# Chunked attention and a capacity-limited expert layer: wider rows for queries, keys and values, and zeros written beside the attention

## The chip, the cores and the metric

The kernel runs on one core of one Trainium2 chip. The metric is the device time of one execution in microseconds (us), here the median of three executions. Inside the core, TensorE (PE in the profile; its weight loads are PEld) multiplies and transposes, VectorE (DVE), ScalarE (ACT) and GpSimd (POOL) copy and compute elementwise, and SyncE (SP) issues nearly all transfers. The transfers run on 16 DMA engines.

## The reference

Two stages, in float32. The first is attention in chunks of 32 queries, each over 8 memory tokens and a window of up to 56 tokens; the second sends each token to its best expert, of 8, and keeps at most 80 tokens an expert.

```python
# q, k, v: (4, 8, 768, 64); mem_k, mem_v: (4, 8, 8, 64); per chunk c of 32 tokens:
k_full = concat(mem_k, k[max(0, 32c - 16) : min(768, 32c + 40)])      # v_full likewise
out[chunk c] = softmax(q_c @ k_full.T / 8) @ v_full
# x: (3072, 512), the heads of a token side by side
logits = x @ w_gate; e = argmax(logits); gw = softmax(logits)[e]
# of the tokens of expert e the 80 with the largest gw are kept
out[kept] = gw * (relu(x[kept] @ w1[e]) @ w2[e])                      # all other rows are zero
```

Since at most 640 of the 3,072 rows get a value, the kernel writes zeros to the whole output first and scatters the kept rows over them.

## The kernel before

**Tiling of the attention.** There are 16 pairs of heads, each with 768 tokens. A pair is done in two halves of 384 tokens, which makes 32 units (`units`, `NU`). A unit has four groups of 96 queries (`GQ`, `NG`), three chunks each, and a group sees 128 keys (`WK`): 8 of the memory and 120 tokens. So the values of a unit are, for each of two heads and four groups, 128 rows (8 of memory, 120 of tokens) of 64 numbers and a one; the one makes the sum of the weights come out of the same matmul.

**Loading.** `load_q` and `load_k` bring a pair's 768 tokens in as 96 partitions of eight tokens (`T0`), for two heads, so each partition gets two runs of 2,048 bytes. GpSimd copies that into the order in which TensorE can turn it (`kh`, L318; `qh`, L294), TensorE turns it (L330, L301), and VectorE or ScalarE moves the result from PSUM to `kT` and `qT` (L335, L304). Since the windows begin 16 tokens before a group and the memory takes eight, a key's first column lies two partitions over; one of four transposes uses a shifted identity (`shift`) for this. `load_v` brings in rows 8 to 127 of `vw` (L250), one transfer a head, in rows of 64 numbers or 256 bytes. Ahead of this GpSimd sets the ones (L242) and copies the memory's values into rows 0 to 7 (L243).

**Order.** The loop over `NU` units is written out. In step i TensorE makes the scores of unit i+1 (L765), turns a coming pair's keys or queries, turns the result of unit i-1 (L364), and multiplies unit i by its values (L346). Between these lie pieces of the ranking of tokens (`steps`), one a step. `in_order` fixes the order on every engine as it is written. SP's transfers are in that order too: in step i, the keys or queries two pairs on, the values of unit i+6, a finished block of `x` to DRAM (`xd`, L370), and, in three of four steps from i = 4 on, a piece of 512 KB of expert weights (L184, from the list `slow`, 20 pieces of five weights).

**After the attention** come the rest of the ranking, which fills `idx_g` and `idx_s`, then the eight experts. SP writes the zeros behind the last block of `x`: 12 pieces of 512 KB (`nothing`, L194), then the weights that are still missing, 44 pieces. Both go through `paced`, which keeps three pieces under way. The 16 expert weights have nine places (`WR`); the loads from w9 on wait for a matmul to leave their place. `run_experts` gathers an expert's rows of `xd` (L924), turns them (L936), multiplies by the first weight (L957) and the second (L971), and scatters the rows (L1019).

Of the kernel before, what the change touches and what calls it, by code (L numbers as in the profile page):

```python
# [12 lines left out]
F32 = mybir.dt.float32  # L13
# [5 lines left out]
PSUM = bass.MemoryType.PSUM  # L19

CHUNK = 32
LEFT = 16
RIGHT = 8
GQ = 96
NG = 4
HT = NG * GQ
T0 = 8
JG = GQ // T0
MS = 8
WK = 128  # L30
# [4 lines left out]
def _ap(ap, extra, dims):  # L35
    return bass.AP(tensor=ap.tensor, offset=ap.offset + extra, ap=dims)
# [26 lines left out]
def kernel(  # L63
# [13 lines left out]
    nc = tc.nc  # L77
    B, H, S, D = q.shape
# [13 lines left out]


    WR, WR0, WR2 = 9, 2, 2
    assert D == 64 and G == 2 * NG and NC == 96 and HT % 128 == 0 and mem_k.shape[2] == MS == T0
# [13 lines left out]
    xd = dram.tile([N, DM], F32, name="xd")  # L109

    ident = const.tile([128, 128], F32, name="ident")
    shift = const.tile([NC + 2, NC + 2], F32, name="shift")
# [88 lines left out]
    class Attention:  # L201


        def __init__(self, es, ps_t, ld):
            self.ld, self.nld = ld, 0
            self.ps_t = ps_t
            pool = es.enter_context(tc.tile_pool(name="at", bufs=1))
            self.io = es.enter_context(tc.tile_pool(name="io", bufs=2))
            self.mem = pool.tile([128, NP, T0], F32, name="mem")
            self.qs, self.ks, self.qT, self.kT, self.vw, self.mv = {}, {}, {}, {}, {}, {}  # L210
            self.kh = pool.tile([NC + 2, T0, 2, D], F32, name="kh")
            nc.gpsimd.memset(self.kh[NC : NC + 2], 0.0)

        def room(self):

            self.nld += 1
            return self.ld[:NC, self.nld % 4, :].rearrange("p (e x) -> p e x", e=2)

        def load_q(self, n):
            if n >= NP:  # L220
# [12 lines left out]
        def load_v(self, n, f):  # L233

            b, h = n // HP, 2 * (n % HP)
            vw = self.vw[n, f] = self.io.tile([128, 2, NG, D + 1], F32, name="vw", tag="vw", bufs=8)
            edge = f * (NG - 1) if (n, f) in ((0, 0), (NP - 1, 1)) else None
            if edge is not None:

                r = slice(96, 128) if f else slice(0, 32)  # L240
                nc.gpsimd.memset(vw[r, :, edge, :D], 0.0)
            nc.gpsimd.memset(vw[:, :, :, D], 1.0)  # L242
            nc.gpsimd.tensor_copy(  # L243
                vw[:MS, :, :, :D], self.mv[b][:, h : h + 2].unsqueeze(2).to_broadcast([MS, 2, NG, D])
            )
            t0 = HT * f - LEFT
            if edge is None:

                for e in range(2):
                    nc.sync.dma_start(  # L250
                        vw[MS:, e, :, :D], _ap(v[b, h + e], t0 * D, [[D, WK - MS], [GQ * D, NG], [1, D]])
                    )
                return
            g0 = int(edge == 0)
            for e in range(2):
                nc.sync.dma_start(
                    vw[MS:, e, g0 : g0 + NG - 1, :D],
                    _ap(v[b, h + e], (t0 + GQ * g0) * D, [[D, WK - MS], [GQ * D, NG - 1], [1, D]]),
                )
            t1 = t0 + GQ * edge  # L260
            lo, rows = MS + max(0, -t1), min(S, t1 + WK - MS) - max(0, t1)
            nc.sync.dma_start(
                vw[lo : lo + rows, :, edge, :D], _ap(v[b, h], max(0, t1) * D, [[D, rows], [SD, 2], [1, D]])
            )

        def load_mv(self, b):
# [1 line left out]
            nc.sync.dma_start(self.mv[b], _ap(mem_v[b, 0], 0, [[D, MS], [MS * D, H], [1, D]]))  # L268

        def load_mem(self, queue):  # L270
            mk = self.mk = self.io.tile([NP, T0, 2, D], F32, name="mk", tag="kT", bufs=5)
            for e in range(2):
                queue.dma_start(
                    mk[:, :, e, :], _ap(mem_k, e * MS * D, [[2 * MS * D, NP], [D, T0], [1, D]])
                )

        def turn_mem(self):

            pt = self.ps_t.tile([128, T0, NP], F32, name="pm", tag="t")
            for t in range(T0):  # L280
                nc.tensor.transpose(
                    pt[:, t, :], self.mk[:, t].rearrange("p e d -> p (e d)"), ident[:NP, :NP]
                )
            nc.vector.tensor_copy(self.mem, pt.rearrange("p t n -> p n t"))

        def turn_q(self, n, copies=(nc.gpsimd.tensor_copy,)):
            if n >= NP:
                return
            qT = self.qT[n] = self.io.tile([128, S], F32, name="qT", tag="qT", bufs=5)

            qh = self.io.tile([NC, T0, 2, D], F32, name="qh", tag="turn", bufs=1)
            for e, copy in enumerate(copies):
                c = slice(0, 2) if len(copies) == 1 else slice(e, e + 1)
                copy(  # L294
                    qh.rearrange("p t e d -> p e t d")[:, c],
                    self.qs[n].rearrange("p e (t d) -> p e t d", d=D)[:, c],
                )
            for t0 in range(0, T0, 4):
                pt = self.ps_t.tile([128, 4, NC], F32, name="pq", tag="t")
                for t in range(4):  # L300
                    nc.tensor.transpose(  # L301
                        pt[:, t, :], qh[:, t0 + t].rearrange("p e d -> p (e d)"), ident[:NC, :NC]
                    )
                nc.scalar.copy(  # L304
                    qT.rearrange("p (x t) -> p x t", t=T0)[:, :, t0 : t0 + 4], pt.rearrange("p t x -> p x t")
                )

        def put_mk(self, n):
# [4 lines left out]
        def turn_k(self, n, spread=nc.gpsimd.tensor_copy):  # L313
            if n >= NP:
                return
            kT = self.kT[n] = self.io.tile([128, G, WK], F32, name="kT", tag="kT", bufs=5)
            kh = self.kh
            spread(  # L318
                kh[:NC].rearrange("p t e d -> p e t d"), self.ks[n].rearrange("p e (t d) -> p e t d", d=D)
            )  # L320
            if n:
                self.put_mk(n)
            win = kT[:, :, MS:].rearrange("p g (j t) -> p g j t", t=T0)
            for t0 in range(0, T0, 4):


                pt = self.ps_t.tile([128, 512], F32, name="pk", tag="t")
                for t in range(4):
                    lo, rows = 2 * (t > 0), NC + (2, 0, 0, 1)[t]
                    nc.tensor.transpose(  # L330
                        pt[:, NC * t + lo : NC * t + lo + rows],
                        kh[:rows, t0 + t].rearrange("p e d -> p (e d)"),
                        (shift if t == 0 else ident)[:rows, :rows],
                    )
                nc.vector.tensor_copy(  # L335
                    win[:, :, :, t0 : t0 + 4],
                    _ap(pt, 0, [pt.ap[0], [JG, G], [1, (WK - MS) // T0], [NC, 4]]),
                )

        def values(self, n, f, P, out):  # L340
# [347 lines left out]
    W.given[WR0] = wpool.tile([128, 4, F], F32, name="ld", tag=f"w{WR0}", bufs=1)  # L688

    with ExitStack() as actx:  # L690
        ps_t = actx.enter_context(tc.tile_pool(name="ps_t", bufs=2, space=PSUM))
# [13 lines left out]
        at.load_mv(0)  # L705
        at.load_v(0, 0)
        make_identity(nc, ident)
        nc.gpsimd.tensor_copy(shift[:, 2:], ident[: NC + 2, :NC])
        nc.gpsimd.tensor_copy(shift[:, :2], ident[: NC + 2, NC : NC + 2])
# [116 lines left out]
        at.load_q(3)  # L826
        at.load_v(0, 1)
        at.load_v(1, 1)
        for i in range(NU):
            n, f = units[i]  # L830
            r = i // HP
# [20 lines left out]
            if later:  # L852
                later.popleft()()
            if i == NU - 2:
                lp = ps_t.tile([128, 512], F32, name="lp", tag="t")
# [199 lines left out]
    with tc.If(redo[1] > 0):  # L1055

        with ExitStack() as actx:
            wk = actx.enter_context(tc.tile_pool(name="wk2", bufs=2))
            gt = actx.enter_context(tc.tile_pool(name="gt2", bufs=1))
            ps_t = actx.enter_context(tc.tile_pool(name="ps_t2", bufs=2, space=PSUM))  # L1060
            ps_s = actx.enter_context(tc.tile_pool(name="ps_s2", bufs=2, space=PSUM))
# [8 lines left out]
            for i, (n, f) in enumerate((HP * b + c, f) for b in range(B) for f in range(2) for c in range(HP)):  # L1070
# [3 lines left out]
                if (c, f) == (0, 0):  # L1074
                    at.load_mv(n // HP)
                at.load_v(n, f)
                at.turn_k(n)
                if n == 0:
                    at.put_mk(n)
# [81 lines left out]
```

## Time and profile before

The time is 297.03 us (296.72 to 298.4 in three executions). The profiled execution spans 299.7 us.

| Engine | busy, us | share |
|---|---|---|
| PE | 249.9 | 83% |
| PEld | 217.6 | 73% |
| DVE | 107.6 | 36% |
| POOL | 88.9 | 30% |
| ACT | 81.7 | 27% |

An engine's share is an average over stages that differ, so it says little by itself. Three stages can be told apart by what the engines do: the attention to about 170 us, the end of the ranking to about 187 us, and the experts to the end. By transfer, the largest in the profile are 60 loads of weights of 512 KB, 60 loads of values of 120 KB, 16 of keys and 16 of queries of 384 KB, 12 pieces of zeros of 512 KB and 8 blocks of `xd` of 768 KB. The median time from issue to landing is 8.5 us for values and 6.6 us for keys.

### The profile page before, as it was taken

The page shows a single profiled execution, that of the slowest core. Times are in us where ns is not written, and L with a number is a line of the kernel's source. Part 1 is how long each engine was busy: PE and PEld are TensorE (multiplying, and loading weights), DVE is VectorE, ACT ScalarE, POOL GpSimd, SP SyncE. Part 2 cuts the span into 40 slices and gives each one's busy share as a digit, 9 for nine tenths or more (in the row PEclk, how much of TensorE's full clock was granted, in tenths as well). Part 3 has the DMA queues.
Part 4 walks back from the last instruction along what each step waited for, and adds up shares of the span by engine and source line. Part 5 has one row for each costly group of instructions (what it writes and reads, how often), then busy time and mean ns, then how long its engine had stood idle before and what let it go on. Part 6 is the DMA issues. An engine that isn't in the chain of part 4 may idle for free. (4 is left out here: it accounts for less than half of the span.)

```text
span 299.7 us, 11347 instructions
## 1 busy us (share of the span) xinstructions
PE 249.9 (83%) x5007; PEld 217.6 (73%) x5007; DVE 107.6 (36%) x282; ACT 81.7 (27%) x197; POOL 88.9 (30%) x209
## 2 busy tenths in 40 slices
PE   6799799777999796999799966999898939695980
PEld 6698688656887584887688844999897829695970
DVE  1232324745649443749365763010210101010030
ACT  2224145445455263365455410110010001010100
POOL 3566563614728125337011024110210200010121
PEclk9958879999799798799999965699999978997996
DMA  7999999999999999999937198998989989884001
GB/s 186 232 210 226 225 198 252 215 229 269 208 290 210 208 288 208 184 283 213 274 116 247 73 378 293 368 312 264 338 281 340 288 308 333 302 321 148 26 24 31
DMA packets 60454, 70.43 MB, mean 235 GB/s; under 512 B 34909, under 2 KB 34941, under 8 KB 60397
## 3 DMA queue, kind: packets, MB, share of 16 engines
q1 hardware_dynamic: 58381, 66.65, 85.5%
q0 software_dynamic: 1056, 2.62, 2.7%
q8 instruction: 41, 0.67, 1.0%
q10 hardware_dynamic: 960, 0.36, 0.6%
q14 instruction: 16, 0.13, 0.2%
HBM read 55.72 MB, written 13.89 MB: 232 GB/s over the span
## 5 line engine op out<-in xcount | busy, mean ns | idle before, releaser
L957 PE MATMUL hp<-xn,w 128*64 128x80 f32 x896 | 40.2, 255 | 12.1 <-DMA w<-in_moe_w_dram 9.9
L957 PEld LDWEIGHTS hp<-xn,w 128*64 128x64 f32 x896 | 37.8, 155 | 14.0 <-DMA w<-in_moe_w_dram 11.2
L765 PE MATMUL sp<-qT,kT 64*128 64x96 f32 x512 | 36.2, 282 | 5.5 <-issue 5.2
L773 ACT ACTIVATE P<-sp 128x384 f32<-128x384 f32 x64 | 28.0, 488 | 41.8 <-PE sp L765 41.8
L765 PEld LDWEIGHTS sp<-qT,kT 64*128 64x128 f32 x512 | 35.9, 202 | 3.8 <-issue 3.2
L346 PE MATMUL o<-vw,P 128*32 128x65 f32 x1536 | 32.5, 235 | 6.0 <-issue 4.1
L971 PE MATMUL yt<-hT,w 128*64 128x80 f32 x896 | 34.3, 234 | 1.9 <-issue 1.9
L346 PEld LDWEIGHTS o<-vw,P 128*32 128x32 f32 x1536 | 26.3, 118 | 12.7 <-issue 10.6
L971 PEld LDWEIGHTS yt<-hT,w 128*64 128x64 f32 x896 | 32.3, 137 | 4.0 <-issue 3.9
L961 ACT ACTIVATE hT<-hp 128x320 f32<-128x320 f32 x16 | 7.0, 438 | 98.7 <-PE hp L957 98.7
L1019 POOL DMA_INDIRECT out_dram<-y,idx_s x7 | 6.5, 934 | 81.9 <-DVE y L1018 66.5
L335 DVE COPY kT<-pk 128x480 f32<-128x480 f32 x32 | 19.8, 654 | 24.7 <-PE pk L330 24.6
L243 POOL COPY vw<-mv 8x512 f32<-8x512 f32 x32 | 20.6, 644 | 14.6 <-DMA mv<-in_mem_v_dram 14.6
L938 DVE COPY xn<-xp 128x320 f32<-128x320 f32 x8 | 3.9, 492 | 50.9 <-PE xp L936 50.9
L318 POOL COPY kh<-ld 96x1024 f32<-96x1024 f32 x15 | 15.5, 1035 | 18.3 <-PE more L534 6.6
L443 POOL TENSOR_TENSOR desc<-oh,masks 128x24 bf16<-128x24 bf16 x16 | 3.3, 228 | 58.9 <-DVE over_s L353 39.7
L516 DVE SCALAR_TENSOR_TENSOR less<-gbs,gw,behind 128x384 bf16<-128x384 f32 x21 | 19.2, 944 | 0.0
L301 PE MATMUL pq<-ident,qh 96*128 96x96 f32 x128 | 16.8, 283 | 2.4 <-POOL qh L294 2.1
L355 DVE TENSOR_TENSOR xr<-o,over_s 128x384 f32<-128x384 f32 x32 | 17.8, 558 | 1.1
L364 PE MATMUL xt<-ident,xr 128*128 128x128 f32 x96 | 17.9, 299 | 0.0
L294 POOL COPY qh<-ld 96x1024 f32<-96x1024 f32 (+1 forms) x16 | 16.4, 1028 | 4.1 <-DMA ld<-in_q_dram 4.1
L304 ACT COPY qT<-pq 128x384 f32<-128x384 f32 x32 | 14.4, 489 | 11.6 <-PE pq L301 11.4
(150 smaller groups left out, 330.7 us busy)
## 6 DMA issues: line engine op xcount, KB each, us to landing
w<-in_moe_w_dram SPq DMA_DIRECT2D x60, 512.0 KB, 5.8
vw<-in_v_dram SPq DMA_DIRECT2D x60, 120.0 KB, 8.5
ld<-in_k_dram SPq DMA_DIRECT2D x16, 384.0 KB, 6.6
ld<-in_q_dram SPq DMA_DIRECT2D x16, 384.0 KB, 6.7
xd<-xr SPq DMA_DIRECT2D x8, 768.0 KB, 7.3
out_dram<-zero SPq DMA_DIRECT2D x12, 512.0 KB, 5.1
ld<-in_moe_w_dram SPq DMA_DIRECT2D x4, 512.0 KB, 6.6
vw<-in_v_dram SPq DMA_DIRECT2D x4, 90.0 KB, 5.9
```

The source lines that it names most:

```text
L243: nc.gpsimd.tensor_copy(vw[:MS, :, :, :D], self.mv[b][:, h : h + 2].unsqueeze(2).to_broadcast([MS, 2, NG, D]))
L294: copy(qh.rearrange("p t e d -> p e t d")[:, c], self.qs[n].rearrange("p e (t d) -> p e t d", d=D)[:, c],)
L301: nc.tensor.transpose(pt[:, t, :], qh[:, t0 + t].rearrange("p e d -> p (e d)"), ident[:NC, :NC])
L335: nc.vector.tensor_copy(win[:, :, :, t0 : t0 + 4], _ap(pt, 0, [pt.ap[0], [JG, G], [1, (WK - MS) // T0], [NC, 4]]),)
L346: nc.tensor.matmul(out[32 * i : 32 * i + 32, e, t, :], lhsT=P[e][:, g, CHUNK * c : CHUNK * c + CHUNK], rhs=self.vw[n, f][:, e, g, :], star ...
L355: nc.vector.tensor_tensor(out=xr[:, :, 128 * c : 128 * c + 128].rearrange("p t (e d) -> p e t d", e=2), in0=o[:, :, :, :D], in1=over_s[:, ...
L364: nc.tensor.transpose(xt[:, 128 * t : 128 * t + 128], xr[:, t, 128 * c : 128 * c + 128], ident)
L516: nc.vector.scalar_tensor_tensor(out=self.less[:, i, :], in0=self.gb, scalar=self.gw[:, i : i + 1], in1=behind[:, 128 * (NT - 1 - i) : 128 ...
L765: nc.tensor.matmul(sp[e][:, g], lhsT=at.kT[n][r, NG * f + g, :], rhs=at.qT[n][r, HT * f + GQ * g : HT * f + GQ * g + GQ], start=False, sto ...
L773: nc.scalar.activation(P[i][e], sp[e], Act.Exp, scale=scale)
L957: nc.tensor.matmul(hp[j : j + 64, f, :], lhsT=w1[:, c, f1 : f1 + 64], rhs=xns[e][:, c, :], start=c == 0, stop=c == DK - 1,)
L971: nc.tensor.matmul(yt[j : j + 64, d, :], lhsT=w2[:, f, d * 128 + j : d * 128 + j + 64], rhs=hTs[e][:, f, :], start=f == 0, stop=f == FK - 1,)
```

## The change

There are four edits. Six tokens a partition (`T0 = 6`) make 128 partitions of keys and queries, with runs of 1,536 bytes, and three transposes a PSUM tile instead of four. The shift of the keys goes into the column at which a transpose writes, so `shift` is gone, and two fixed PSUM tiles `pt`, zeroed once, take the place of a rotating pair. The values come in as 128 rows, eight more than before, which lie under the memory's; the memory's values are copied over them afterwards, by `put_mv`, two steps ahead of use. The ones are written once, into eight fixed tiles (`rooms`). And in the steps from i = 4 on that issue no piece of weights, a piece of zeros is issued.

```diff
-T0 = 8
+T0 = 6
...
+            self.pt = [ps_t.tile([128, 512], F32, name=f"pt{i}", bufs=1) for i in range(2)]
+            for pt in self.pt:
+                nc.vector.memset(pt, 0.0)
...
-            self.kh = pool.tile([NC + 2, T0, 2, D], F32, name="kh")
-            nc.gpsimd.memset(self.kh[NC : NC + 2], 0.0)
+            self.kh = pool.tile([NC, T0, 2, D], F32, name="kh")
+            self.rooms = [pool.tile([128, 2, NG, D + 1], F32, name=f"vw{i}") for i in range(8)]
+            for vw in self.rooms:
+                nc.gpsimd.memset(vw[:, :, :, D], 1.0)
...
-            nc.gpsimd.memset(vw[:, :, :, D], 1.0)
-            nc.gpsimd.tensor_copy(
-                vw[:MS, :, :, :D], self.mv[b][:, h : h + 2].unsqueeze(2).to_broadcast([MS, 2, NG, D])
-            )
-            t0 = HT * f - LEFT
...
-                        vw[MS:, e, :, :D], _ap(v[b, h + e], t0 * D, [[D, WK - MS], [GQ * D, NG], [1, D]])
...
+            t0 = HT * f - LEFT - MS
...
+                    vw[:, e, g0:g1, :D],
+                    _ap(v[b, h + e], (t0 + GQ * g0) * D, [[D, WK], [GQ * D, g1 - g0], [1, D]]),
...
+        def put_mv(self, n, f):
+            b, h = n // HP, 2 * (n % HP)
+            nc.gpsimd.tensor_copy(
+                self.vw[n, f][:MS, :, :, :D],
+                self.mv[b][:, h : h + 2].unsqueeze(2).to_broadcast([MS, 2, NG, D]),
             )
...
-            for t0 in range(0, T0, 4):
-                pt = self.ps_t.tile([128, 4, NC], F32, name="pq", tag="t")
-                for t in range(4):
+            for t0 in range(0, T0, 3):
+                pt = self.pt[t0 // 3][:, 3 : 3 + 3 * NC].rearrange("p (t x) -> p t x", t=3)
+                for t in range(3):
...
-            for t0 in range(0, T0, 4):
...
-                pt = self.ps_t.tile([128, 512], F32, name="pk", tag="t")
-                for t in range(4):
-                    lo, rows = 2 * (t > 0), NC + (2, 0, 0, 1)[t]
+            for u0, step in ((0, NC), (3, NC + 1)):
...
+                pt = self.pt[u0 // 3]
+                for i in range(3):
+                    c = 3 + i * step - (u0 + i > 3)
                     nc.tensor.transpose(
-                        pt[:, NC * t + lo : NC * t + lo + rows],
-                        kh[:rows, t0 + t].rearrange("p e d -> p (e d)"),
-                        (shift if t == 0 else ident)[:rows, :rows],
+                        pt[:, c : c + NC], kh[:, (u0 + i + 2) % T0].rearrange("p e d -> p (e d)"), ident
                     )
...
         at.load_v(1, 1)
+        at.put_mv(*units[0])
+        at.put_mv(*units[1])
         for i in range(NU):
...
                 constants[i]()
+            if i + 2 < NU:
+                at.put_mv(*units[i + 2])
...
             if (i >= NU - 6 or i >= 4 and i % 4 < 3) and slow:
                 slow.popleft()()
+            elif i >= 4:
+                nothing.popleft()()
```

More of the change, by code (lines that the diff above doesn't have):

```diff
@@ L94 @@
     WR, WR0, WR2 = 9, 2, 2
-    assert D == 64 and G == 2 * NG and NC == 96 and HT % 128 == 0 and mem_k.shape[2] == MS == T0
+    assert D == 64 and G == 2 * NG and NC == 128 and HT % 128 == 0 and mem_k.shape[2] == MS
     assert N == B * S and DM == H * D and E == 8 and HP == DK == 4
@@ L111 @@
     ident = const.tile([128, 128], F32, name="ident")
-    shift = const.tile([NC + 2, NC + 2], F32, name="shift")
     masks = const.tile([128, mask_np.shape[1]], BF16, name="masks")
@@ L204, in __init__ @@
         def __init__(self, es, ps_t, ld):
-            self.ld, self.nld = ld, 0
-            self.ps_t = ps_t
+            self.ld, self.nld, self.nv = ld, 0, 0
+            self.pt = [ps_t.tile([128, 512], F32, name=f"pt{i}", bufs=1) for i in range(2)]
+            for pt in self.pt:
+                nc.vector.memset(pt, 0.0)
             pool = es.enter_context(tc.tile_pool(name="at", bufs=1))
             self.io = es.enter_context(tc.tile_pool(name="io", bufs=2))
-            self.mem = pool.tile([128, NP, T0], F32, name="mem")
+            self.mem = pool.tile([128, NP, MS], F32, name="mem")
             self.qs, self.ks, self.qT, self.kT, self.vw, self.mv = {}, {}, {}, {}, {}, {}
-            self.kh = pool.tile([NC + 2, T0, 2, D], F32, name="kh")
-            nc.gpsimd.memset(self.kh[NC : NC + 2], 0.0)
+            self.kh = pool.tile([NC, T0, 2, D], F32, name="kh")
+            self.rooms = [pool.tile([128, 2, NG, D + 1], F32, name=f"vw{i}") for i in range(8)]
+            for vw in self.rooms:
+                nc.gpsimd.memset(vw[:, :, :, D], 1.0)
         def room(self):
             self.nld += 1
-            return self.ld[:NC, self.nld % 4, :].rearrange("p (e x) -> p e x", e=2)
+            return self.ld[:NC, self.nld % 4, : 2 * T0 * D].rearrange("p (e x) -> p e x", e=2)
         def load_q(self, n):
@@ L235, in load_v @@
             b, h = n // HP, 2 * (n % HP)
-            vw = self.vw[n, f] = self.io.tile([128, 2, NG, D + 1], F32, name="vw", tag="vw", bufs=8)
+            vw = self.vw[n, f] = self.rooms[self.nv % 8]
+            self.nv += 1
             edge = f * (NG - 1) if (n, f) in ((0, 0), (NP - 1, 1)) else None
@@ L241, in load_v @@
                 nc.gpsimd.memset(vw[r, :, edge, :D], 0.0)
-            nc.gpsimd.memset(vw[:, :, :, D], 1.0)
-            nc.gpsimd.tensor_copy(
-                vw[:MS, :, :, :D], self.mv[b][:, h : h + 2].unsqueeze(2).to_broadcast([MS, 2, NG, D])
-            )
-            t0 = HT * f - LEFT
-            if edge is None:
-                for e in range(2):
-                    nc.sync.dma_start(
-                        vw[MS:, e, :, :D], _ap(v[b, h + e], t0 * D, [[D, WK - MS], [GQ * D, NG], [1, D]])
-                    )
-                return
+            t0 = HT * f - LEFT - MS
             g0 = int(edge == 0)
+            g1 = NG - int(edge == NG - 1)
             for e in range(2):
                 nc.sync.dma_start(
-                    vw[MS:, e, g0 : g0 + NG - 1, :D],
-                    _ap(v[b, h + e], (t0 + GQ * g0) * D, [[D, WK - MS], [GQ * D, NG - 1], [1, D]]),
-                )
[L260 to L263, printed above, removed]
+                    vw[:, e, g0:g1, :D],
+                    _ap(v[b, h + e], (t0 + GQ * g0) * D, [[D, WK], [GQ * D, g1 - g0], [1, D]]),
+                )
+            if edge is not None:
+                t1 = t0 + GQ * edge
+                lo, rows = max(0, -t1), min(S, t1 + WK) - max(0, t1)
+                nc.sync.dma_start(
+                    vw[lo : lo + rows, :, edge, :D], _ap(v[b, h], max(0, t1) * D, [[D, rows], [SD, 2], [1, D]])
+                )
+        def put_mv(self, n, f):
[3 more added lines that the diff above has]
+                self.mv[b][:, h : h + 2].unsqueeze(2).to_broadcast([MS, 2, NG, D]),
             )
@@ L270, in load_mem @@
         def load_mem(self, queue):
-            mk = self.mk = self.io.tile([NP, T0, 2, D], F32, name="mk", tag="kT", bufs=5)
+            mk = self.mk = self.io.tile([NP, MS, 2, D], F32, name="mk", tag="kT", bufs=5)
             for e in range(2):
                 queue.dma_start(
-                    mk[:, :, e, :], _ap(mem_k, e * MS * D, [[2 * MS * D, NP], [D, T0], [1, D]])
+                    mk[:, :, e, :], _ap(mem_k, e * MS * D, [[2 * MS * D, NP], [D, MS], [1, D]])
                 )
         def turn_mem(self):
-            pt = self.ps_t.tile([128, T0, NP], F32, name="pm", tag="t")
-            for t in range(T0):
+            pt = self.pt[1][:, : MS * NP].rearrange("p (t n) -> p t n", t=MS)
+            for t in range(MS):
                 nc.tensor.transpose(
@@ L297, in turn_q @@
                 )
-            for t0 in range(0, T0, 4):
-                pt = self.ps_t.tile([128, 4, NC], F32, name="pq", tag="t")
-                for t in range(4):
-                    nc.tensor.transpose(
-                        pt[:, t, :], qh[:, t0 + t].rearrange("p e d -> p (e d)"), ident[:NC, :NC]
-                    )
+            for t0 in range(0, T0, 3):
+                pt = self.pt[t0 // 3][:, 3 : 3 + 3 * NC].rearrange("p (t x) -> p t x", t=3)
+                for t in range(3):
+                    nc.tensor.transpose(pt[:, t, :], qh[:, t0 + t].rearrange("p e d -> p (e d)"), ident)
                 nc.scalar.copy(
-                    qT.rearrange("p (x t) -> p x t", t=T0)[:, :, t0 : t0 + 4], pt.rearrange("p t x -> p x t")
+                    qT.rearrange("p (x t) -> p x t", t=T0)[:, :, t0 : t0 + 3], pt.rearrange("p t x -> p x t")
                 )
@@ L318, in turn_k @@
             spread(
-                kh[:NC].rearrange("p t e d -> p e t d"), self.ks[n].rearrange("p e (t d) -> p e t d", d=D)
+                kh.rearrange("p t e d -> p e t d"), self.ks[n].rearrange("p e (t d) -> p e t d", d=D)
             )
@@ L323, in turn_k @@
             win = kT[:, :, MS:].rearrange("p g (j t) -> p g j t", t=T0)
-            for t0 in range(0, T0, 4):
-                pt = self.ps_t.tile([128, 512], F32, name="pk", tag="t")
-                for t in range(4):
-                    lo, rows = 2 * (t > 0), NC + (2, 0, 0, 1)[t]
+            for u0, step in ((0, NC), (3, NC + 1)):
+                pt = self.pt[u0 // 3]
+                for i in range(3):
+                    c = 3 + i * step - (u0 + i > 3)
                     nc.tensor.transpose(
-                        pt[:, NC * t + lo : NC * t + lo + rows],
-                        kh[:rows, t0 + t].rearrange("p e d -> p (e d)"),
-                        (shift if t == 0 else ident)[:rows, :rows],
+                        pt[:, c : c + NC], kh[:, (u0 + i + 2) % T0].rearrange("p e d -> p (e d)"), ident
                     )
                 nc.vector.tensor_copy(
-                    win[:, :, :, t0 : t0 + 4],
-                    _ap(pt, 0, [pt.ap[0], [JG, G], [1, (WK - MS) // T0], [NC, 4]]),
+                    win[:, :, :, u0 : u0 + 3],
+                    _ap(pt, 0, [pt.ap[0], [JG, G], [1, (WK - MS) // T0], [step, 3]]),
                 )
@@ L690 @@
     with ExitStack() as actx:
-        ps_t = actx.enter_context(tc.tile_pool(name="ps_t", bufs=2, space=PSUM))
+        ps_t = actx.enter_context(tc.tile_pool(name="ps_t", bufs=1, space=PSUM))
         ps_s = actx.enter_context(tc.tile_pool(name="ps_s", bufs=2, space=PSUM))
@@ L707 @@
         make_identity(nc, ident)
-        nc.gpsimd.tensor_copy(shift[:, 2:], ident[: NC + 2, :NC])
-        nc.gpsimd.tensor_copy(shift[:, :2], ident[: NC + 2, NC : NC + 2])
         nc.gpsimd.memset(wgc, 0.0)
@@ L854 @@
             if i == NU - 2:
-                lp = ps_t.tile([128, 512], F32, name="lp", tag="t")
+                lp = at.pt[0]
                 nc.tensor.matmul(lp[:, : NT * E], lhsT=zerob, rhs=zerob[:, : NT * E], start=True, stop=False)
@@ L1060 @@
             ps_t = actx.enter_context(tc.tile_pool(name="ps_t2", bufs=2, space=PSUM))
-            ps_s = actx.enter_context(tc.tile_pool(name="ps_s2", bufs=2, space=PSUM))
+            ps_s = actx.enter_context(tc.tile_pool(name="ps_s2", bufs=1, space=PSUM))
             ps_o = actx.enter_context(tc.tile_pool(name="ps_o2", bufs=1, space=PSUM))
@@ L1076 @@
                 at.load_v(n, f)
+                at.put_mv(n, f)
                 at.turn_k(n)
```

## The prediction

> **What bounds the kernel now.** I read the page's DMA rows first, then the busy time by stage, then the timelines of TensorE and SP in the stage where those disagree, then GpSimd's.
>
> ```profile
> PEclk9958879999799798799999965699999978997996
> DMA  7999999999999999999937198998989989884001
> GB/s 186 232 210 226 225 198 252 215 229 269 208 290 210 208 288 208 184 283 213 274 116 247 73 378 293 368 312 264 338 281 340 288 308 333 302 321 148 26 24 31
> DMA packets 60454, 70.43 MB, mean 235 GB/s; under 512 B 34909, under 2 KB 34941, under 8 KB 60397
> ```
>
> A digit is a slice of 7.5 us. The DMA engines are full in the attention (slices 2 to 20) at only 184 to 290 GB/s, nearly idle in slices 21 to 23, and full again at about 300 GB/s for the experts. So there is a hole of some 20 us in a resource that is short on both sides of it.
>
> ```profile
> core 0: us, PE busy (x) PEld busy (x) DVE busy (x) ACT busy (x) POOL busy (x), PEclk, DMA share, GB/s
> 28.00:157.00 129.00, 112.57 (x2300) 93.40 (x2300) 69.49 (x180) 59.27 (x145) 54.82 (x139) 0.92 1.06 228
> 190.00:280.00 90.00, 75.88 (x1810) 71.28 (x1807) 10.06 (x20) 6.57 (x15) 8.56 (x9) 0.93 0.86 288
> ```
>
> In the attention PE is busy 112.57 of 129 us and the DMA share is over 1[...]: two limits lie close together. In the experts PE is idle 14 us of 90, while all else but DMA rests. What ends that idle time is in PE's timeline (start, duration, what ran, and in brackets the idle time before it with its releaser):
>
> ```profile
> 244.07 0.53 PE L957 MATMUL hp<-xn,w 128*64 128x80 f32 x4 [3.14 <-DMA w<-in_moe_w_dram]
> 245.26 0.54 PE L957 MATMUL hp<-xn,w 128*64 128x80 f32 x4 [0.66 <-DMA w<-in_moe_w_dram]
> 246.53 5.92 PE L957 MATMUL hp<-xn,w 128*64 128x80 f32 x116 [0.73 <-DMA w<-in_moe_w_dram]
> 258.92 0.36 PE L957 MATMUL hp<-xn,w 128*64 128x80 f32 x4 [0.75 <-DMA w<-in_moe_w_dram]
> 260.81 4.23 PE L957 MATMUL hp<-xn,w 128*64 128x80 f32 x116 [1.53 <-DMA w<-in_moe_w_dram]
> 272.68 0.36 PE L957 MATMUL hp<-xn,w 128*64 128x80 f32 x4 [1.91 <-DMA w<-in_moe_w_dram]
> 274.21 5.74 PE L957 MATMUL hp<-xn,w 128*64 128x80 f32 x116 [1.17 <-DMA w<-in_moe_w_dram]
> ```
>
> The first weight matrices of the last three experts come late: the waits add to 9.89 us. After two of them the same 116 matmuls take 5.92 and 5.74 instead of 4.23 us, since the clock fell (6 in PEclk): 3.2 us more. So late weights cost **13.1 us**. Why they are late is in SP's timeline:
>
> ```profile
> 170.43 19.82 SPq L194 DMA_DIRECT2D out_dram<-zero  x12
> 191.05 78.15 SPq L184 DMA_DIRECT2D w<-in_moe_w_dram  x44
> ```
>
> The twelve pieces of zeros hold the queue for 19.82 us, 1.65 us each, ahead of every remaining weight; those then come at 78.15/44 = 1.78 us a piece. One stall in the attention concerns the change too:
>
> ```profile
> 73.18 0.73 POOL L243 COPY vw<-mv 8x512 f32<-8x512 f32 x1 [3.00 <-DMA mv<-in_mem_v_dram]
> 73.86 1.03 POOL L294 COPY qh<-ld 96x1024 f32<-96x1024 f32 x1
> 74.95 0.88 PE L301 MATMUL pq<-ident,qh 96*128 96x96 f32 x8 [2.13 <-POOL qh L294]
> ```
>
> GpSimd's copy of the memory's values waits for `mv`; the queries' copy queues behind it, and TensorE waits for that.
>
> [...]in its packet records the 2,048-byte packets take 127 ns on average in 28 to 150 us and 87 ns at 170 to 190, where zeros go out from 128 partitions. [...]in the attention PE stops six times for 0.4 to 3.0 us on "issue" in the middle of a group of matmuls[...].
>
> **The change part by part.** Where a sum has both ends, both go into the range.
>
> Zeros. From i = 4 on, the steps without a piece of weights are 7, 11, 15, 19, 23, 25 (the first 16 pieces are used up), 30 and 31: eight pieces move and four stay. The last three are issued after unit 31's values (145 us) and fall into the hole: free. At the end SP is done with zeros 8 x 1.65 = 13.2 us sooner, at 170.43 + 4 x 1.65 = 177 us. The next weights go into SBUF that the ranking's tiles may hold until about 182.4 us, when its last instruction ends on DVE. So the lead of the weights is between 191.05 - 182.4 = 8.7 and 13.2 us. The last late piece came at 274.2 us; without any stalls PE would want it at about 263 (274.2 less 9.89 of waits and 1.69 of slow matmuls). So about 11 us of lead removes everything, and 8.7 leaves some 2.5 us. Later weights wait for a place: w14 takes that of w5, free at 228 us, and I count it in at about 257 us, so the places don't bind. The gain is 9.5 to 13.1; I take **-12 us**.
>
> The five pieces within the attention add 5 x 256 packets of 2,048 bytes at 87 to 127 ns on 16 engines: 7.0 to 10.2 us of full DMA time.
>
> Queries and keys. A load is 256 packets of 1,536 instead of 192 of 2,048 bytes. On the line between 32 ns (256 bytes, same records) and 127 ns, 1,536 bytes take 100 ns: 32 loads go from 48.8 to 51.2 us, +2.4.[...] I take -5.
>
> Values. [...]averaged over 16 engines 6.7% more packets, at 32 ns some 61 us in all: 0 to +4. I take 0.
>
> So the attention's DMA demand grows by about 8.5 - 5 = 3.5 us, between -5 and +17. Does PE see it? Unit 14's values were issued by 62.6 us and landed 8.3 us later (median) at 70.9. GpSimd would come to `put_mv(14)`, behind `kT` in step 12, at about 82.5: 11.6 us of slack. Keys have more. So a small surplus is hidden[...]: **+1.5 us**.
>
> `put_mv`. A new wait: behind it on GpSimd is the next copy of keys or queries, and TensorE's transposes wait for those. With the slack above it costs nothing in the loop. It takes the place of the wait for `mv`: the stall of 2.13 us above goes, and the slower matmuls after it (xt 0.90 for 0.49, o 1.53 for 0.89 and those behind them, 1.5 us together). The two other waits for `mv` (3.3 and 4.85 us) lie beside "issue" stalls of PE that end as late: nothing. I take **-3 us**.
>
> Start. Four copies of memory values (0.60 us each) stand before the keys' copy at 13.49 us, for which PE idles 1.00 us and then runs at clock 0.73. They go behind it. But `put_mv(1)` then waits for values issued at 10.77 (landing about 19), and the next copy is needed for PE at 20.4. Two PSUM memsets come before the first matmuls, and the wait for `shift` goes. **-1.5 us** (0 to -2.5).
>
> Transposes. Queries: 8 x 83 to 6 x 110 ns by the spacing of matmul starts, nothing. Keys: 0.74 us for eight to six at 110 ns, 0.08 us, 16 times: **-1 us**. GpSimd's copies shrink with their elements (1.03 to about 0.78 us), and 32 memsets go: hidden, since GpSimd is idle 70%.
>
> Sum: -12 + 1.5 - 3 - 1.5 - 1 = -16; I round the small gains down to 15.5: 297.0 - 15.5 = **281.5 us**.
>
> **The rivals.** A: the attention becomes DMA-bound. For it: DMA never rests there. Against: 11 us of slack. With +8 instead of -4: 297 - 12 + 8 = 293. B: the weights' lead is lost, to SBUF that isn't free or to the nine places; then the experts give -6 and the attention -2: 289. C, slower: zeros at 127 ns[...], values at 6.7% more: +17 of DMA, all of it seen, since `put_mv` holds GpSimd[...]; the end gives only its lower bound of -9.5 and the small gains stay (-5.5): 297 + 17 - 9.5 - 5.5 = 299. D: [...]the attention, which loses its stalls: 275.
>
> **How the numbers follow.** 0.57 for the forecast (278 to 286), A 0.15, B 0.13, C 0.09, D 0.06. Reaching into A, B and D gives 275.5 to 293. Faster: the forecast, B, D and most of A, 0.87; within 0.5%: 0.04; slower: C, 0.09.
>
> **What would show it.** SP's zeros after 170 us are four, not twelve, and the weights follow by 182 us; L957's waits for weights fall from 9.9 us to under 2; POOL's waits for `mv` vanish and no longer ones for `vw` appear; the attention ends 2 to 6 us sooner. I am wrong if the experts still wait for weights, or if GpSimd waits over 5 us for values, or if PE's issue stalls grow.

## The result, and the profile after

The changed kernel takes **265.18 us** (261.76 to 265.68, four runs) against 297.71 us (296.72 to 302.32); the ratio is 0.8893, 95% interval 0.8794 to 0.8991. The forecast was 281.5 us, with 275.5 as the lower end: right in direction, but the gain is twice the 15.5 us that were forecast. Slower executions are left out of ratios and of the times in the table below, but the traces of the kernel before (301.62 us) and of e6 (278.19 us) are of such. The page of the profiled execution, of 263.6 us, in slices of 6.6 us:

```profile
PEclk9999999999999999999999557699999999999996
DMA  7999899999999999979192999979999998970110
GB/s 236 283 279 283 220 266 345 351 362 332 365 329 340 356 322 366 316 217 341 70 307 87 378 319 307 304 277 322 298 315 295 310 310 245 344 251 26 30 42 20
DMA packets 64598, 70.96 MB, mean 269 GB/s; under 512 B 37004, under 2 KB 45228, under 8 KB 64540
```

The DMA engines are as busy in the attention as before, but in slices 7 to 17 at 316 to 366 GB/s, where it was 184 to 290. PEclk stands at 9 through the attention, without the 7s and 8s of before. By stage (columns as before):

```profile
28.00:130.00 102.00, 97.84 (x2163) 81.54 (x2163) 64.28 (x176) 57.67 (x141) 46.98 (x108) 1.00 1.00 308
```

PE is busy 97.84 of 102 us, at full clock; it was 112.57 of 129 us at 0.92. SP's timeline, with the last store of `xd` before the change as the first line, and the group of the experts' first matmuls:

```profile
170.01 0.38 SPq L370 DMA_DIRECT2D xd<-xr  x1
```

```profile
144.15 0.38 SPq L370 DMA_DIRECT2D xd<-xr  x1
144.58 5.03 SPq L193 DMA_DIRECT2D out_dram<-zero  x4
150.46 82.21 SPq L183 DMA_DIRECT2D w<-in_moe_w_dram  x44
```

```profile
L961 PE MATMUL hp<-xn,w 128*64 128x80 f32 x896 | 35.0, 241 | 2.1 <-issue 1.5
```

Four pieces of zeros are left, the weights follow at once, and no wait for `w` remains (9.9 us before).

Two marks split the gain. From the first to the last unit's values (the first matmul of each, L346) it is 122.0 us instead of 144.1; the first comes at 20.4 instead of 24.1 us. From the last store of `xd` to the end it is 119.5 us instead of 129.7. So the attention, start included, gave some 26 us and the end 10.2. The two sum to 36 us, since the trace before is of a longer execution; the medians differ by 32.5. The forecast had 4 and 12. Hence the question of the experiments: what made the attention so much faster?

### The profile page after: what moved, and what is told of

Same layout as the page of the kernel before. It is cut to its first block, busy times and chain, and to the rows that moved or that the text cites. A ratio compares the mean times of both kernels' runs of the same rounds, so it can differ in the third digit from the quotient of the medians.

```text
span 263.6 us, 11283 instructions
## 1 busy us (share of the span) xinstructions
PE 232.0 (88%) x4943; PEld 202.7 (77%) x4943; DVE 104.4 (40%) x284; ACT 82.7 (31%) x197; POOL 80.3 (30%) x182
## 5 line engine op out<-in xcount | busy, mean ns | idle before, releaser
L771 ACT ACTIVATE P<-sp 128x384 f32<-128x384 f32 x64 | 27.9, 488 | 30.6 <-PE sp L763 30.6
L961 PE MATMUL hp<-xn,w 128*64 128x80 f32 x896 | 35.0, 241 | 2.1 <-issue 1.5
L961 PEld LDWEIGHTS hp<-xn,w 128*64 128x64 f32 x896 | 34.2, 144 | 2.5 <-issue 1.6
L346 PE MATMUL o<-vw,P 128*32 128x65 f32 x1536 | 28.7, 221 | 0.1
L346 PEld LDWEIGHTS o<-vw,P 128*32 128x32 f32 x1536 | 23.3, 109 | 5.6 <-issue 5.1
L335 DVE COPY kT<-pt 128x480 f32<-128x480 f32 x32 | 19.9, 668 | 18.0 <-PE pt L332 12.0
L305 ACT COPY qT<-pt 128x384 f32<-128x384 f32 x32 | 16.4, 580 | 8.4 <-PE pt L304 8.4
L355 DVE TENSOR_TENSOR xr<-o,over_s 128x384 f32<-128x384 f32 x32 | 17.8, 557 | 1.1
L366 ACT COPY xT<-xt 128x384 f32<-128x384 f32 x32 | 15.6, 489 | 4.3 <-PE xt L364 4.3
L981 DVE COPY ys<-yt 128x320 f32<-128x320 f32 x7 | 3.4, 492 | 32.4 <-PE yt L975 32.4
L319 POOL COPY kh<-ld 128x768 f32<-128x768 f32 x15 | 12.4, 825 | 12.0 <-issue 9.2
L304 PE MATMUL pt<-ident,qh 128*128 128x128 f32 x96 | 14.6, 283 | 1.1 <-DVE kT L335 1.1
```

What stands on the lines that cost most here:

```text
L304: nc.tensor.transpose(pt[:, t, :], qh[:, t0 + t].rearrange("p e d -> p (e d)"), ident)
L305: nc.scalar.copy(qT.rearrange("p (x t) -> p x t", t=T0)[:, :, t0 : t0 + 3], pt.rearrange("p t x -> p x t"))
L335: nc.vector.tensor_copy(win[:, :, :, u0 : u0 + 3], _ap(pt, 0, [pt.ap[0], [JG, G], [1, (WK - MS) // T0], [step, 3]]),)
L346: nc.tensor.matmul(out[32 * i : 32 * i + 32, e, t, :], lhsT=P[e][:, g, CHUNK * c : CHUNK * c + CHUNK], rhs=self.vw[n, f][:, e, g, :], star ...
L355: nc.vector.tensor_tensor(out=xr[:, :, 128 * c : 128 * c + 128].rearrange("p t (e d) -> p e t d", e=2), in0=o[:, :, :, :D], in1=over_s[:, ...
L366: nc.scalar.copy(xT, xt[:, :HT])
```

## The experiments

The theories: **rows** (96 rows of keys and 120 of values slow the DMA, 128 don't), with the rivals **computation** (fewer transposes, shorter copies, no wait for `mv`) and **packets** (the size of a packet counts). A load of keys or queries is said to have 96 or 128 rows by the partitions that it fills. "Values" below is the stretch from the first to the last unit's values, and "gaps" the sum of PE's pauses over 0.15 us in it. GB/s is the rate from 28 to 120 us. The 256-byte packet's mean time is from the trace's packet records, 28 to 150 us.

| kernel | time, us | values, us | gaps, us | GB/s | 256 B, ns |
|---|---|---|---|---|---|
| before | 297.03 | 144.1 | 16.6 | 233 | 32 |
| e1 zeros moved | 293.50 | 147.8 | 13.4 | 256 | 29 |
| e2 values in 128 rows | 292.14 | 136.1 | 11.4 | 253 | 28 |
| e3 keys and queries in 128 rows | 279.78 | 126.3 | 6.6 | 280 | 24 |
| e4 both, no zeros moved | 274.41 | 120.6 | 3.6 | 296 | 19 |
| after | 265.18 | 122.0 | 4.9 | 320 | 19 |
| e6 after, keys in 96 + 32 | 274.41 | 132.2 | 11.1 | 275 | 26 |
| e7 after, values in 120 + 8 | 273.90 | 126.4 | 9.1 | 280 | 22 |
| e8 before, `mv` early | 298.12 | 136.9 | 13.7 | 253 | 29 |
| e10 before, weights later (one execution) | 309.21 | 126.8 | 8.4 | 206 | 26 |
| e11 after, 11 MB more | 276.11 | 131.7 | 13.1 | 349 | 19 |
| e13 e3, keys in 96 + 32 | 293.93 | 140.6 | 16.1 | 247 | 29 |
| e14 after, longer copies | 265.57 | 123.1 | 4.4 | 314 | 19 |

Everything but the time is from one trace of each kernel. The kernel before was run again beside each group of experiments. Beside e1 to e4 one of its seven runs counts (292.5 us; all lie between 292.5 and 305.0), so these four are compared with each other and by their traces. Beside the others the runs that count took 297.5 to 302.5 us, so times of different groups compare only roughly.

**e1: the zeros alone.**

```diff
             if (i >= NU - 6 or i >= 4 and i % 4 < 3) and slow:
                 slow.popleft()()
+            elif i >= 4:
+                nothing.popleft()()
```

> The kernel before, with the eight pieces of zeros moved beside the attention and nothing else. Both theories agree on the end: the weights lead by some 13 us and the experts lose about 10 us. They also agree that the attention, whose DMA rate stays near 228 GB/s without wider rows, gets five pieces more (about 8 to 10 us of DMA time). If the DMA limits the attention, it gets 5 to 10 us longer and the total is 290 to 296 us; if its slack hides them, as I predicted, the total is about 286 us.

SP's timeline of e1:

```profile
171.29 0.38 SPq L370 DMA_DIRECT2D xd<-xr  x1
171.73 5.04 SPq L194 DMA_DIRECT2D out_dram<-zero  x4
177.61 2.44 SPq L184 DMA_DIRECT2D w<-in_moe_w_dram  x2
```

The weights start 6.3 instead of 21.0 us after the last store of `xd`, and the end from that store on takes 118.7 us instead of 129.7: -11.0. The values take 3.7 us more. So by the traces the move alone is worth some 7 us beside narrow rows; the times (293.50 us, against that one run of 292.5) don't resolve it.

**e2 and e3: each kind of wide rows alone; e4: both without the zeros.** e2 puts `rooms`, `put_mv` and the 128-row `load_v` into the kernel before, e3 `T0 = 6` with all that follows from it; e4 is the changed kernel without the two lines of e1.

> The kernel before, with values alone loaded as 128 rows and the memory's copied over them afterwards (96 partitions of keys and queries, zeros at the end). Theory V, that the 120 rows of the values slow the DMA: 256-byte packets fall from 32 to about 20 ns, the issue stalls of PE go, the total is 272 to 280 us. Theory K, that the 96 rows of keys and queries do: only the wait for mv goes, 292 to 296 us, packets of 256 bytes stay near 30 ns.

> The kernel before, with keys and queries alone as 128 partitions of six tokens (values in 120 rows, zeros at the end). Theory V: little, 292 to 297 us, 256-byte packets stay near 30 ns. Theory K: 272 to 280 us, and those packets fall to about 20 ns too[...].

> The changed kernel with the zeros left at the end, so both row changes without the move. Both theories: the attention as in the changed kernel or 0 to 3 us shorter, the experts again late by the zeros: 10 to 13 us more than the changed kernel, 273 to 278 us. If the zeros cost nothing in the attention and the weights' lead is worth what I predicted, exactly 12 us more than the changed kernel.

Both parts count, the keys for more: the values' stretch falls by 8.0 us (e2), 17.8 us (e3) and 23.5 us (e4) against the trace before. The 8.0 us alone would not show it, since e8, whose time is as before, differs from that trace by 7.2 us; and e2's time is what theory K forecast. But between e3 and e4, which add the values to wide keys, the time falls from 279.78 to 274.41 us, and no run of one reaches into those of the other. So theory V fails, and K falls short. The stretch is 1.4 us longer after than in e4, by the zeros or by chance (e12, with the same attention as after, has 120.7); the end takes 128.5 us in e4 and 119.5 after, so the weights' lead is worth 9.0.

**e6, e7, e13: the same computation with the rows cut.** In e6 and e13:

```diff
-            nc.sync.dma_start(self.ks[n], _ap(k[b, h], 0, [[T0 * D, NC], [SD, 2], [1, T0 * D]]))
+            for r0, r1 in ((0, 96), (96, 128)):
+                nc.sync.dma_start(
+                    self.ks[n][r0:r1], _ap(k[b, h], r0 * T0 * D, [[T0 * D, r1 - r0], [SD, 2], [1, T0 * D]])
+                )
```

and the same for queries; e7 cuts the values at row 120 in this way.

> The changed kernel with each load of keys or queries cut into rows 0 to 95 and 96 to 127: the same bytes, packets and computation, only the rows of a transfer differ. Theory rows: the gain of the wider keys goes for the most part, the attention's 256-byte packets rise from 19 to 24 ns or more, 275 to 287 us. Theory computation (shorter copies on GpSimd and fewer transposes make the gain): 264 to 268 us, as the changed kernel.

> The changed kernel with each load of values cut into rows 0 to 119 and 120 to 127, which doubles the number of value transfers. Theory rows: the attention loses what the values' part gave beside wide keys (e3 to e4, 6.5 us), 269 to 275 us. Theory computation (the wait for mv and the ones written once make that part): 264 to 268 us.

> As e3 (keys and queries alone as 128 partitions of six tokens), with each of their loads cut into rows 0 to 95 and 96 to 127: the same bytes, packets and computation as e3. Theory rows: the 20.8 us of e3 go for the most part, first to last values 136 to 146 us instead of 126, total within 8 us of the kernel before. Theory computation: as e3, first to last values 124 to 129 us, 18 to 22 us less than before.

e13 differs from e3 only in the rows of a transfer and, since each load is now two, in their number. The stretch from 28 to 120 us, e3 first, then e13:

```profile
28.00:120.00 92.00, 86.38 (x1831) 70.82 (x1829) 57.37 (x149) 50.01 (x121) 47.02 (x126) 0.98 1.09 280
```

```profile
28.00:120.00 92.00, 78.45 (x1579) 64.86 (x1578) 48.53 (x128) 42.97 (x102) 40.43 (x112) 0.93 1.14 247
```

PE got through 1,831 matmuls in one and 1,579 in the other; the DMA share is higher in the slower one. Of the 17.8 us that the values' stretch lost in e3, 14.3 are back in e13 (140.6 us, where theory computation had 124 to 129). Its ratio is 0.9799 (0.9671 to 0.9926), so some 6 us of gain over the kernel before are left. e6 (0.914, 0.896 to 0.932) and e7 (0.911, 0.897 to 0.925) lose some 6 to 7 us of the changed kernel's gain by the ratios, whose intervals just touch that of the changed kernel. For e6 this is well short of the 17.7 us between e2 and e4, of which its theory had most. All but the time in e6's row is rough. A cut also doubles the number of transfers, and no run doubles it with the rows kept whole, so these three don't separate the two, and computation is not wholly excluded as the source of e3's gain; e9 and e15 below have narrow loads that are not cut.

**e14: GpSimd's time back, the rows kept.** A memset of 256 elements stands before each of GpSimd's copies of keys and queries:

```diff
...
             kh = self.kh
+            nc.gpsimd.memset(self.pad, 0.0)
             spread(
```

> The changed kernel with a memset of 256 elements on GpSimd ahead of every copy of keys and of queries, which makes these about as long as before the change (1.03 us for 0.83). Theory rows: 264 to 268 us, as the changed kernel. Theory computation: GpSimd's time was on the path of the attention, 4 us or more are lost, 269 us or more.

265.57 us, ratio 0.8818 (0.8731 to 0.8905): unchanged, though a memset takes 0.30 us and with a copy of 0.83 us more than a copy did before (1.03). So the length of GpSimd's copies is not on the path. The transposes are not put back here; e3 and e13 have the same ones.

**e5, e9, e15: the loads by themselves.** A stretch is, for instance, `stage(K(96, 512, 12))`: twelve loads of 96 rows and two runs of 512 numbers; `mixed(K(...), V(8, 120, 24))` puts two loads of value rows 8 to 127 behind each.

> The disputed loads by themselves: 13 stretches of 6 to 28 loads of some 3 MB, nothing else running, each stretch begun when the one before has landed (no attention and no experts, the output is all zeros). In order: keys as 96 rows of 2 x 2,048 bytes, as 128 rows of 2 x 1,536, as 96 rows of 2 x 1,536, as 128 rows of 2 x 2,048; values as rows 8 to 127 (120), 0 to 127 (128), 16 to 127 (112), 0 to 119 (120) and 0 to 95 (96), in runs of 256 bytes; then one key load and two value loads in turn: 96 with 120, 128 with 128, 96 with 128, 128 with 120. Theory rows[...]: 96 rows of either packet size stay at 210 to 270 GB/s and 128 rows of either at 300 to 370; values at 128 rows 10 to 40% above 120 and 112. Theory packets (size alone): the order follows 2,048 and 1,536 bytes, so the old keys are the faster. Theory mixture: each alone runs at its full rate, and only 96 with 120 in turn falls to some 220 GB/s.

In e5 the stretches ran into one another, so it isn't read. e9 fixed the order, but the output's write fell into its first key stretch, and in e15 into the last one (96 with 120 again), so these two aren't read.

> The disputed loads by themselves once more, now in a fixed order, each stretch begun only when all of the one before has landed (no attention, no experts, the output is all zeros). After a short first stretch: 12 key loads each as 96 rows of 2 x 2,048 bytes, 128 rows of 2 x 1,536, 96 of 2 x 1,536, 128 of 2 x 2,048; 28 value loads each as rows 8 to 127, 0 to 127, 16 to 127, 0 to 95; then 12 key and 24 value loads in turn: 96 with 120 rows, 128 with 128, 96 with 128, 128 with 120. Theory rows: 96 rows of either packet size reach at most 80% of the rate of 128 rows, and in turn 96 with 120 at most 75% of 128 with 128. Theory packets: the rate follows the packet's size whatever the rows.[...]

> The key loads by themselves again, the output written last (no attention, no experts, the output is all zeros). After a short first stretch: 12 loads each as 96 rows of 2 x 2,048 bytes, 128 of 2 x 1,536, 96 and 32 rows of 2 x 1,536 in two transfers, again 96 and again 128; then 12 key and 24 value loads in turn: 96 with 120, 128 with 120, 96 with 128, 128 with 128, 128 with 120, 96 with 120. Theory rows: 96 rows at 80 to 90% of 311 GB/s, and the cut loads no better; in turn only 128 with 128 above 250 GB/s, as in e9. If 128 with 120 comes out above 96 with 120 by over 8% both times, the first measurement of it was off and rows explain e3; if not, the loads alone do not explain it.

e15, with windows set to each stretch (the last three columns are clock, DMA share and GB/s): in order keys in 96 rows, 128, 96 + 32, 96, 128, then 96 with 120, 128 with 120, 96 with 128, 128 with 128.

```profile
6.10:24.90 18.80, 0.00 (x0) 0.00 (x0) 1.00 0.97 251
28.60:43.20 14.60, 0.00 (x0) 0.00 (x0) 1.00 0.94 323
46.80:66.40 19.60, 0.00 (x0) 0.00 (x0) 1.00 1.05 241
70.00:90.00 20.00, 0.00 (x0) 0.00 (x0) 1.00 1.02 236
94.10:108.80 14.70, 0.00 (x0) 0.00 (x0) 1.00 0.94 322
112.40:147.10 34.70, 0.00 (x0) 0.00 (x0) 1.00 1.13 221
155.00:190.30 35.30, 0.00 (x0) 0.00 (x0) 1.00 1.12 217
198.10:231.40 33.30, 0.00 (x0) 0.00 (x0) 1.00 1.16 236
239.60:267.70 28.10, 0.00 (x0) 0.00 (x0) 1.00 1.11 280
```

The same 4.72 MB take 18.8 and 20.0 us in 96 rows and 14.6 and 14.7 us in 128, although the 128 rows have the smaller packets. By the means, 19.4 and 14.65 us, 128 rows need 76% of the time; the bytes that a row gets in a load fall to 75%, from 4,096 to 3,072. Whether the one follows from the other, no trace shows. From e9, uncut, 96 rows with packets of 1,536 bytes and 128 rows with 2,048:

```profile
63.40:77.10 13.70, 0.00 (x0) 0.00 (x0) 1.00 1.02 258
80.80:98.20 17.40, 0.00 (x0) 0.00 (x0) 1.00 0.98 362
```

So 96 rows are the slower ones at either packet size, 258 against 323 GB/s (80%) and 251 or 236 against 362 (65 to 69%); and in 128 rows the larger packets are the faster, 362 against 323. The change made packets smaller, so packets don't explain its gain. The cut loads bring the same packets into the same 128 rows and still run at 241 GB/s; whether it is the rows of each part or the number of transfers stays open. A DMA share near 1 says nothing on the rate: it is 1.02 at 236 and 0.94 at 323 GB/s. From e9, values in rows 8 to 127, 0 to 127 and 16 to 127:

```profile
101.80:120.40 18.60, 0.00 (x0) 0.00 (x0) 1.00 1.16 186
127.10:143.90 16.80, 0.00 (x0) 0.00 (x0) 1.00 1.21 219
150.50:166.30 15.80, 0.00 (x0) 0.00 (x0) 1.00 0.98 203
```

28 loads of 128 rows are done in less time than 28 of 120, in one stretch of each. The 112 rows lie between by rate, at 203 GB/s between 186 and 219; why, no run shows. In turn, only 128 with 128 is fast: 28.1 against 34.7 us (27.9 against 34.6 in e9). One thing stays open: in turn, wide keys beside 120-row values gain nothing over the 221 of narrow ones (217, and in a second stretch the line below), yet in the kernel they do (e3), and e13 loses it when they are cut.

```profile
275.50:309.30 33.80, 0.00 (x0) 0.00 (x0) 1.00 1.07 227
```

So the loads alone do not explain e3. What lies between them in the kernel (weights, stores) was not tried with them.

**e10 and e11: the load itself.** e10 moves all 20 pieces of weights in `slow` out of the attention of the kernel before (its text below counts 16); e11 reads 21 pieces more in the changed one:

```diff
...
+            if 4 <= i < 25:
+                nc.sync.dma_start(junk[i % 3], moe_w1[i % 8, :128, :])
```

> The kernel before, with the 16 pieces of weights that it loads beside the attention (8.4 MB) put behind it instead, ahead of the zeros. The experts then start late, so the total is longer, 305 to 325 us, and only the attention is to be read. If full DMA engines cause PE's issue stalls and its slow clock, the stretch from the first to the last unit's values falls from 144 to 118 to 128 us, with 96 and 120 rows as they are. If the uneven rows do this whatever the load, it stays at 140 us or more.

> The changed kernel, with 21 more loads of 512 KB (even rows of 128, read into tiles that nobody uses) beside the attention, so 11 MB more there; the output is unchanged. If it is the DMA's load that stops PE, at about 320 GB/s they add up to 34 us of DMA time of which some 15 to 20 was free: the attention gets 10 to 20 us longer with issue stalls as in the kernel before, 275 to 287 us in all. If only uneven rows stop PE, 264 to 268 us.

With less to load, narrow rows give 126.8 us; with more, wide rows give 131.7. The stretch from 28 to 120 us in the kernel before, e10 and e11:

```profile
28.00:120.00 92.00, 77.75 (x1542) 64.63 (x1540) 46.04 (x118) 40.81 (x99) 43.12 (x108) 0.91 1.11 233
28.00:120.00 92.00, 84.60 (x1837) 70.54 (x1834) 57.90 (x145) 47.31 (x118) 51.81 (x128) 1.00 0.94 206
28.00:120.00 92.00, 84.05 (x1827) 69.61 (x1823) 54.09 (x145) 49.74 (x120) 40.24 (x92) 1.00 1.07 349
```

Among PE's waits, "issue" is one for which the view sees no cause (us in total, times, longest). In the kernel before, in e10, in the changed kernel and in e11:

```profile
PE sp L765 <- issue: 5.2, 2, 3.0
PE o L346 <- issue: 4.1, 3, 2.1
```

```profile
PE o L346 <- issue: 2.7, 2, 2.2
```

```profile
PE sp L763 <- issue: 1.8, 2, 1.3
```

```profile
PE o L346 <- issue: 5.4, 7, 1.5
PE sp L764 <- issue: 1.8, 2, 1.0
```

In the values' stretch such stalls sum to 9.3, 2.7, 1.8 and 8.5 us. So with either kind of rows they follow the DMA's load. That rows matter since they set how long the same bytes keep the DMA loaded is my reading of this with e15 (19.4 against 14.65 us). What such a stall waits for, the view does not say. The page of the kernel before names a queue of instructions (packets, MB, share of 16 engines):

```profile
q8 instruction: 41, 0.67, 1.0%
```

In the values' stretches of the 13 traces of the table all 68 such stalls end 1.3 to 1.8 us after a packet of this queue has landed, though one lands only every 6 to 7 us. That PE stood waiting for that packet is my reading; no run isolates it.

PE's clock does not follow the load: it is 1.00 in e11 as in e10. In the trace of the kernel before it stood at half four times between 35 and 124 us, for 20.5 us in all, each time next to a pause of PE of 2.1 to 3.0 us; e11's longest pause there is 1.5 us. But pauses of 2.2 us in e10 and of 2.5 us in e8 had no such effect, so what lowers the clock stays open.

**e8: the memory's values early.** `load_mv` is issued eight units sooner, with four buffers.

> The kernel before, with the memory's values of a batch loaded eight units sooner, so that GpSimd never waits for them; nothing else. As I predicted: the stall of 2.1 us and the slow matmuls after it go, 3 us less than before, the waits of GpSimd for mv fall from 14.6 to under 4 us (the first stays). Rival: DMA sets the pace of the attention and the stall comes back elsewhere: no change, within 1.5 us.

The ratio is 0.9929 (0.9801 to 1.0056), which holds both theories: inconclusive. GpSimd's waits for `mv` fell from 14.6 to 3.4 us.

**e12: an attempt at more.** `busy(wait, 8)` for `busy(wait, 4)`.

> The changed kernel with eight instead of four spare matmuls (of 256 columns) while TensorE waits for the first gathered rows[...]. In the changed kernel it idles 4.45 us there and the first 128 matmuls of the experts take 6.88 instead of 4.65 us. If the idle time lowers the clock, up to 2.2 us less than the changed kernel, 262 to 264 us; if the clock is low already, as PEclk shows from 150 us on, no change within 1 us.

PE's timeline of e12:

```profile
162.06 0.47 PE L940 MATMUL xp<-ident,xg 80*128 80x80 f32 x4 [2.95 <-DMA xg<-xd,idx_g]
163.11 6.29 PE L961 MATMUL hp<-xn,w 128*64 128x80 f32 x128 [0.58 <-DVE xn L942]
```

The first 128 matmuls of the experts take 6.29 instead of 6.88 us. The time is 263.71 us, ratio 0.8787 (0.8689 to 0.8884), which can't be told from the changed kernel's.

## Why the prediction was right or wrong

**Zeros: right at the end.** The weights' lead is 21.0 - 6.3 = 14.7 us; the forecast had 8.7 to 13.2. The buffers did not hold it up: the weights start 6.3 us after the store. The end gave 10.2 for 12, within 9.5 to 13.1: PE now waits 4.45 us for the first gathered rows instead of 2.59, and no run shows why. What the five pieces cost in the attention is not resolved: the traces have 1.4 us beside wide rows and 3.7 beside narrow ones, but traces of nearly the same attention differ as much (120.7 us in e12, 123.1 in e14).

**`put_mv`: right.** The only wait for `vw` on GpSimd is 0.5 us. **Transposes: not resolved.** Without gaps the values' stretch is 118.4 us in e10 and 117.0 in e4, both at full clock, but 118.6 in e11, which has the transposes of e4; the forecast was 1 us. **Start:** 3.7 for 1.5, but e1, with the old start, has its first values at 21.7 us, so 1.3 is as well supported. **The `mv` stall:** -3 was not resolved (e8).

**Failed: the price of the rows.** For keys and queries I took -5 within -12 to +2.4. Alone, twelve loads went from 19.4 to 14.65 us (means of two), which is -12.7 us for 32: the low end of the range, and no trace stood behind that end. For values I took 0 within 0 to +4, and no trace stood behind the 0; alone, 28 loads went from 18.6 to 16.8 us, -4 us for 64: the sign was wrong. In turn they went from 34.7 to 28.1 us for 12 + 24, or -18 us for all 32 + 64. So by the loads alone the demand fell by some 9 us, zeros included, where the sum had +3.5 and its range began at -5.

**Failed: "Does PE see it?"** I asked only whether tiles would be late, found 11.6 us of slack, and took a change of demand as hidden but for an estimate of 1.5 us, which no number of the trace gave. The runs show -22.1 us in the values' stretch, 11.7 us of gaps (16.6 to 4.9) and 10.4 us of slower matmuls. The issue stalls that I had listed (the view puts down five so, and one of my six to a load of keys) and the clock of 0.92 were what PE already paid, and I booked none of it as recoverable except under rival D (0.06). e10 and e11 show that the issue stalls come and go with the DMA's load. For the clock only e10 does; in e11 the stalls are back and the clock is not lower. Rival D named the outcome, an attention without its stalls; at 275 it was too small as well.

## What to carry to other kernels

Count the rows of every transfer before its bytes: here 128 rows moved the same keys in three quarters of the time of 96 (14.65 against 19.4 us), at smaller packets. A DMA share of 1 is no rate (1.02 came with 236 GB/s, 0.94 with 323); compare GB/s with what the same pattern reaches alone. And where a stage has full DMA engines, look for PE's "issue" stalls and its clock, and price relief there too, not only late tiles: here that was most of 22 us.

## What was not expected of the hardware

Eight more rows of values a load (120 to 128, 6.7% more bytes) took less time, 16.8 for 18.6 us (e9). Loads in turn are fast only when both kinds fill 128 rows: 280 GB/s, against 217 to 236 with either one narrow (e15). And stalls of PE come with DMA load alone: 11 MB more, which nobody reads, took PE's gaps from 4.9 to 13.1 us and the time to 276.1 us, at full clock (e11).
